# Sparse attention in front of a bilinear feed-forward: probabilities as the stationary operand, and x brought back transposed through DRAM

## Chip, cores and metric

One core of a Trainium2 chip. The metric is the device time of one execution, in microseconds (us). Several executions are timed for each kernel, in the same rounds as the kernel before. "Before" and "after" are the two kernels of the change.

## The reference

```python
# q, k, v: 8 batches x 8 heads x 576 positions x 64, float32
scores = q @ k^T / 8
mask   = local (0 <= i - j < 32) for heads 0-3, strided (j <= i and i % 32 == j % 32) for heads 4-7
attn   = softmax(where(mask, scores, -1e9)) @ v
x      = attn.transpose(0, 2, 1, 3).reshape(4608, 512)
out    = ((x @ w_a) * (x @ w_b)) @ w_out          # 512 -> 1536 -> 512, float32 out
```

The feed-forward contracts over the 512 features. TensorE contracts over partitions, so x has to lie in SBUF transposed, features on partitions (`xT`), before its first matmul.

## The kernel before

Keys and queries are transposed on TensorE, then for each of eight units (a pair of heads, half of the positions) come the scores (S), the masked exponentials `p`, and the values (V). Scores come out keys on partitions, so `p` can be the moving operand and V the stationary one; the result then has features on partitions already and goes straight into `xT`. The price is that the sums over keys have to be made by a matmul with ones, so that they are there for all 64 rows of a head.

```python
def step_S(b, u):                      # scores of one unit, two heads at a time in row halves
    ...
    for i, (k0, q0, g) in enumerate(segs):
        for hh in range(2):
            d0 = 64 * hh
            nc.tensor.matmul(st[:M, hh, i * n:(i + 1) * n],
                             lhsT=kT[d0:d0 + 64, c, k0:k0 + M],
                             rhs=qT[d0:d0 + 64, c, q0:q0 + n], start=True, stop=True)
    ...                                # exp on ScalarE, mask by a bitwise AND on VectorE

def step_V(b, u):                      # sums and values, two heads at a time in column halves
    dn = psm.tile(...)
    for hh in range(2):
        nc.tensor.matmul(dn[64 * hh:64 * hh + 64, :W], lhsT=ones[:M], rhs=p[:M, hh], ...)
    o = psm.tile(...)
    for i, (k0, q0, g) in enumerate(segs):
        for hh in range(2):
            nc.tensor.matmul(o[64 * hh:64 * hh + 64, i * n:(i + 1) * n], lhsT=vt,
                             rhs=p[:M, hh, i * n:(i + 1) * n], ...)
    nc.scalar.activation(ln, dn[:, :W], ACT.Ln)
    nc.scalar.activation(rc, ln, ACT.Exp, scale=-1.0)          # 1 / sum
    nc.vector.tensor_mul(xT[...], o[:, :W], rc)

SEQ = (("T0",), ("S0",), ("S1", "T1"), ("V0", "S2"), ...)       # 13 slots
# the feed-forward of tile t (512 tokens: 12 groups of gate matmuls ffn_ab, 4 of output
# matmuls ffn_y), with one slot of the attention of batch t+1 behind each group
```

Batch 0's attention runs ahead of everything, batch b's is woven into tile b-1, and the last two tiles have none. TensorE, SyncE and GpSimd keep the order in which they are written.

The softmax here doesn't subtract the row's maximum and nothing guards it: scores larger than these inputs give would overflow.

## Time and profile before

| | before |
|---|---|
| median of the runs | 375.85 us |
| first gate matmul of tile 0 (start of the feed-forward) | 25.21 us |
| tile 0, tile 1 | 42.56, 40.89 us |
| tiles 2 to 6, each | 39.95 us |
| tiles 7 and 8, without attention | 31.08 us |

A "tile time" here is the distance from one tile's first gate matmul to the next one's, read from the trace's records. The next fence is from the page of the kernel before: busy tenths of TensorE in 40 slices of the span, and the software DMA queue, which carries the loads (packets, MB, share of the 16 engines' time).

```profile
PE   2789999999999999999999999999999999999995
...
q0 software_dynamic: 46512, 19.67, 43.2%
```

There is no hole in TensorE's row after the first 30 us. To save time, TensorE must be given less to do and must not be made to wait.

### The profile page before, as it was taken

How to read it: one execution, taken by the hardware profiler on the slowest of the kernel's cores; microseconds unless marked ns; L12 is line 12 of the kernel's file. 1: busy time of each engine (PE TensorE's matmuls, PEld its weight loads, DVE VectorE, ACT ScalarE, POOL GpSimd, SP SyncE). 2: the span in 40 equal slices, each digit the busy share in tenths (PEclk: the TensorE clock that was granted, in tenths of full speed). 3: DMA queues.
4: the chain of work that ended last, by engine and by line, in shares of the span. 5: the costliest groups of instructions: out<-in, count | busy, mean ns of one | idle time of the engine just before them, and what ended most of it. 6: DMA issues, size and time to landing. Idle time of an engine off the chain costs nothing.

```text
span 374.7 us, 7708 instructions
## 1 busy us (share of the span) xinstructions
PE 358.7 (96%) x3217; PEld 173.8 (46%) x3217; DVE 169.7 (45%) x299; ACT 178.6 (48%) x347; POOL 52.3 (14%) x72
## 2 busy tenths in 40 slices
PE   2789999999999999999999999999999999999995
PEld 2544454455444544444444544554445444444442
DVE  2653652465426652556245643655255513312421
ACT  1563764466526652666246643766166623312320
POOL 7833540013001110103000300000000000000000
PEclk9999999999999999999999999999999999999999
DMA  7999999845644194229414843000200020011002
GB/s 114 155 194 197 205 191 191 177 66 37 98 117 65 8 100 117 53 40 103 93 56 66 72 81 99 2 2 19 94 2 3 1 86 28 0 58 56 0 30 84
DMA packets 51730, 29.59 MB, mean 79 GB/s; under 512 B 28400, under 2 KB 47088, under 8 KB 51696
## 3 DMA queue, kind: packets, MB, share of 16 engines
q0 software_dynamic: 46512, 19.67, 43.2%
q1 hardware_dynamic: 5184, 9.44, 6.9%
q8 instruction: 25, 0.41, 0.4%
q14 instruction: 9, 0.07, 0.1%
HBM read 39.31 MB, written 9.44 MB: 130 GB/s over the span
## 4 chain that ended last, share of the span: by engine, by line
PE 93%; DMA 2%; POOL 1%; ACT 1%; DVE 1%; issue 1%; DVEq 0%; POOLq 0%
PE mm L254 52%; PE mm L265 25%; PE sm L166 5%; PE st L194 4%; PE sm L213 4%; PE sm L220 2%; DMA vl<-in_v_dram 2%; POOL k L116 0%; DVE y_sb L271 0%; POOL msl L73 0%; ACT rc L226 0%; DVE xT L232 0%; ACT ln L224 0%; POOL q L116 0%; PE mm L166 0%
## 5 line engine op out<-in xcount | busy, mean ns | idle before, releaser
L259 DVE TENSOR_TENSOR pf<-a_sb,mm 128x512 bf16<-128x512 f32 x108 | 74.3, 688 | 89.9 <-PE mm L254 89.9
L254 PE MATMUL mm<-xT,wa_sb 128*128 128x512 bf16 x432 | 113.6, 386 | 0.8 <-DVE xT L232 0.8
L254 PE MATMUL mm<-xT,wb_sb 128*128 128x512 bf16 x432 | 111.9, 382 | 0.0
L258 ACT COPY a_sb<-mm 128x512 f32<-128x512 f32 x108 | 63.2, 585 | 70.2 <-PE mm L254 70.2
L265 PE MATMUL mm<-wo_sb,pf 128*128 128x512 bf16 x432 | 96.3, 379 | 0.0
L254 PEld LDWEIGHTS <-wb_sb 128*128 128x128 bf16 x432 | 42.6, 99 | 52.9 <-issue 2.9
L265 PEld LDWEIGHTS <-pf 128*128 128x128 bf16 x432 | 40.9, 98 | 47.9
L254 PEld LDWEIGHTS <-wa_sb 128*128 128x128 bf16 x432 | 36.4, 98 | 38.4 <-issue 1.7
L199 ACT ACTIVATE p<-st 128x576 bf16<-128x576 f32 (+1 forms) x64 | 40.7, 635 | 17.5 <-PE st L194 17.4
L224 ACT ACTIVATE ln<-sm 128x288 f32<-128x288 f32 x64 | 26.3, 410 | 29.5 <-PE sm L213 29.5
L269 ACT COPY y_sb<-mm 128x512 f32<-128x512 f32 x18 | 10.5, 585 | 56.3 <-PE mm L265 56.3
L271 DVE COPY y_sb<-mm 128x512 f32<-128x512 f32 x18 | 12.5, 692 | 52.9 <-PE mm L265 52.9
L232 DVE TENSOR_TENSOR xT<-sm,rc 128x288 bf16<-128x288 f32 x32 | 20.4, 639 | 28.4 <-ACT rc L226 27.8
L226 ACT ACTIVATE rc<-ln 128x288 f32<-128x288 f32 x64 | 28.3, 443 | 2.0
L172 ACT COPY qT<-sm 128x576 bf16<-128x576 bf16 x28 | 17.8, 637 | 13.9 <-PE sm L166 13.9
L194 PE MATMUL st<-qT,kT 64*72 64x72 bf16 (+1 forms) x448 | 21.1, 212 | 0.6 <-ACT p L199 0.5
L213 PE MATMUL sm<-p,ones 72*64 72x288 bf16 (+1 forms) x128 | 21.1, 327 | 0.3 <-DVE p L205 0.3
L229 DVE TENSOR_TENSOR xT<-sm,rc 128x288 bf16<-128x288 f32 x32 | 14.6, 458 | 14.2 <-ACT rc L226 12.5
L116 POOL DMA_DIRECT2D q<-in_q_dram x16 | 11.7, 730 | 58.4 <-PE sm L166 53.7
L213 PEld LDWEIGHTS <-ones 72*64 72x64 bf16 (+1 forms) x128 | 7.3, 110 | 24.6 <-issue 21.2
L166 PEld LDWEIGHTS <-q 72*64 72x64 bf16 (+1 forms) x448 | 11.2, 117 | 15.9 <-issue 8.9
L129 POOL DMA_DIRECT2D vl<-in_v_dram x8 | 11.6, 1454 | 45.9 <-PE st L194 45.4
(41 smaller groups left out, 177.8 us busy)
## 6 DMA issues: line engine op xcount, KB each, us to landing
out_dram<-y_sb SPq DMA_DIRECT2D x36, 256.0 KB, 2.0
q<-in_q_dram POOLq DMA_DIRECT2D x16, 288.0 KB, 6.8
k<-in_k_dram POOLq DMA_DIRECT2D x16, 288.0 KB, 7.9
vl<-in_v_dram POOLq DMA_DIRECT2D x7, 384.0 KB, 6.8
vs<-in_v_dram POOLq DMA_DIRECT2D x8, 288.0 KB, 5.8
wa_sb<-in_moe_w_a_dram POOLq DMA_DIRECT2D x4, 384.0 KB, 11.6
wb_sb<-in_moe_w_b_dram POOLq DMA_DIRECT2D x4, 384.0 KB, 11.7
wo_sb<-in_moe_w_out_dram POOLq DMA_DIRECT2D x4, 384.0 KB, 13.5
```

The costliest lines, as they stand in the source:

```text
L166: nc.tensor.transpose(tp[64 * hh:64 * hh + 64, r, :], src[:, 2 * cc + hh, r, :], ident[:n, :n])
L172: nc.scalar.copy(o, i_)
L194: nc.tensor.matmul(st[:M, hh, i * n:(i + 1) * n], lhsT=kT[d0:d0 + 64, c, k0:k0 + M], rhs=qT[d0:d0 + 64, c, q0:q0 + n], start=True, stop=True)
L199: nc.scalar.activation(p[:M], st[:M, :, :W], ACT.Exp, scale=scale)
L213: nc.tensor.matmul(dn[64 * hh:64 * hh + 64, :W], lhsT=ones[:M], rhs=p[:M, hh], start=True, stop=True)
L224: nc.scalar.activation(ln, dn[:, :W], ACT.Ln)
L226: nc.scalar.activation(rc, ln, ACT.Exp, scale=-1.0)
L232: nc.vector.tensor_mul(dst, o[:, :W].rearrange("d (r p) -> d p r", r=4), rc.rearrange("d (r p) -> d p r", r=4))
L254: nc.tensor.matmul(ps_, lhsT=w[:, f // FC, kk, 128 * (f % FC):128 * (f % FC + 1)], rhs=xT[:, kk, TTOK * t:TTOK * (t + 1)], start=(kk == 0) ...
L258: nc.scalar.copy(a_sb, ab[0])
L259: nc.vector.tensor_mul(pf[:, f, :], a_sb, ab[1])
L265: nc.tensor.matmul(y, lhsT=pf[:, f, 128 * j:128 * (j + 1)], rhs=wo_sb[:, f, :], start=(f == 0), stop=(f == FD - 1))
```

## The change

The intent is to take work off TensorE. The probabilities become the *stationary* operand and V the moving one. V gets a 65th column of ones, so the sums come out as one more column of the result and the matmuls with ones go away. Scores use whole-array matmuls, with queries padded by zeros, in place of row halves; this avoids changes of tiling. (The tiling is how a matmul divides the array: the views print 128\*128 for the whole array, 64\*128 for a row half, 96\*64 for a column half.) Now the result has positions on partitions, so x must be transposed: for batch 0 on TensorE (X), and from batch 1, the second batch, on by writing the normalized rows to DRAM and reading them back through the DMA crossbar, which transposes on the way (W); this gives TensorE no instruction. Batch 1's attention is pressed into tile 0 by running two slots behind some of the groups.

```diff
-    pmm = ... bufs=4 ...   psm = ... bufs=2 ...
+    pmm = ... bufs=3 ...   po = ... bufs=1 ...   ptp = ... bufs=1 ...   # accumulators
+    dram = ctx.enter_context(tc.tile_pool(name="dram", bufs=2, space=bass.MemoryType.DRAM))
 ...
     def load_vs(b):
-        nc.gpsimd.dma_start(out=t, in_=v[b, HL:].rearrange("h (p r) d -> p h r d", r=RS))
+        for h in range(HL):
+            nc.gpsimd.dma_start(out=vs_buf[b % 2][:, h, :, 0:D], in_=v[b, HL + h]...)
 ...
     def step_S(b, u):
-                nc.tensor.matmul(st[...], lhsT=kT[d0:d0 + 64, c, k0:k0 + M], rhs=qT[d0:d0 + 64, c, q0:q0 + n], ...)
+                nc.tensor.matmul(st[...], lhsT=kT[:, c, k0:k0 + M], rhs=qz[j][:, c, q0:q0 + n], ...)
 ...
     def step_V(b, u):
-            nc.tensor.matmul(dn[...], lhsT=ones[:M], rhs=p[:M, hh], ...)
-                nc.tensor.matmul(o[...], lhsT=vt, rhs=p[:M, hh, i * n:(i + 1) * n], ...)
-        nc.scalar.activation(ln, dn[:, :W], ACT.Ln)
-        nc.scalar.activation(rc, ln, ACT.Exp, scale=-1.0)
+                nc.tensor.matmul(ov[:, j, i, :], lhsT=p[:M, j, i * n:(i + 1) * n], rhs=vt, ...)
+        nc.vector.reciprocal(rc[:n, :, :G], ov[:, :, :, D])
+        nc.vector.tensor_mul(dst, ov[:, :, :, 0:D], rc[...].to_broadcast([n, 2, G, D]))
+
+    def step_X(b, c):                  # batch 0: transpose x on TensorE
+        for g in range(S // n):
+            nc.tensor.transpose(tv[:, g, :], x[:, g].rearrange("p j d -> p (j d)"), ident[:n, :n])
+        nc.scalar.copy(dst, tv)
+
+    def step_W(b, z):                  # other batches: write, then transposing read
+        nc.sync.dma_start(out=xd..., in_=x)
+        nc.sync.dma_start_transpose(out=xT[:, 2 * z:2 * z + 2, S * b:S * (b + 1)], in_=xd)
 ...
+            g0 = 2 if b == 1 else 16 * (b - 1) - 2
+            for b, g0, seq in todo:
+                if seq and i >= g0:
+                    run(b, seq.pop(0))
+                    if b == 1 and i in (3, 4, 12):       # doubled slots
+                        run(b, seq.pop(0))
```

The cuts leave out the layout of the buffers and the new slot order (14 slots, with W0 after the first four units and W1 at the end of each batch).

More of the change, by code (lines that the diff above doesn't have):

```diff
@@ L20 @@
 PAD = 32
+VW = 80
 FC = 3
@@ L52 @@
     nat = ctx.enter_context(tc.tile_pool(name="nat", bufs=2))
-    kvp = ctx.enter_context(tc.tile_pool(name="kv", bufs=2))
     sb = ctx.enter_context(tc.tile_pool(name="sb", bufs=3))
     fsb = ctx.enter_context(tc.tile_pool(name="ffn", bufs=3))
-    pmm = ctx.enter_context(tc.tile_pool(name="pmm", bufs=4, space=bass.MemoryType.PSUM))
+    pmm = ctx.enter_context(tc.tile_pool(name="pmm", bufs=3, space=bass.MemoryType.PSUM))
     pst = ctx.enter_context(tc.tile_pool(name="pst", bufs=1, space=bass.MemoryType.PSUM))
-    psm = ctx.enter_context(tc.tile_pool(name="psm", bufs=2, space=bass.MemoryType.PSUM))
+    po = ctx.enter_context(tc.tile_pool(name="po", bufs=1, space=bass.MemoryType.PSUM))
+    dram = ctx.enter_context(tc.tile_pool(name="dram", bufs=2, space=bass.MemoryType.DRAM))
+    ptp = ctx.enter_context(tc.tile_pool(name="ptp", bufs=1, space=bass.MemoryType.PSUM))
     nc.scalar.preload_act_table_set("natural_log_exp_and_others")
     ident = const.tile([128, 128], BF16)
-    ones = const.tile([128, 64], BF16)
+    qz_buf = [[const.tile([128, KD, S], BF16, name=f"qz{i}{j}") for j in range(2)] for i in range(2)]
+    vl_buf = [const.tile([128, HL * 6, VW], BF16, name=f"vl{i}") for i in range(2)]
+    vs_buf = [const.tile([NP, HL, RS, VW], BF16, name=f"vs{i}") for i in range(2)]
     mask_l = const.tile([128, 4, LW], I16)
@@ L74, in select, with consts @@
                                 channel_multiplier=cm)
-    def consts():
-        nc.vector.memset(ones, 1.0)
-        nc.vector.memset(msl, -1.0)
-        for kT in kT_buf:
-            nc.vector.memset(kT[:, 0:2, 0:PAD], 0.0)
+    def consts(i):
+        if i == 0:
+            nc.vector.memset(msl, -1.0)
+        nc.vector.memset(kT_buf[i][:, 0:2, 0:PAD], 0.0)
+        for j in range(2):
+            nc.vector.memset(qz_buf[i][j][64 * (1 - j):64 * (2 - j)], 0.0)
+        nc.vector.memset(vl_buf[i][:, :, D:D + 1], 1.0)
+        nc.vector.memset(vs_buf[i][:, :, :, D:D + 1], 1.0)
+        if i == 0:
+            nc.vector.memset(vl_buf[0][:PAD, 0, 0:D], 0.0)
     def mask_local():
@@ L119, in load_vl @@
     def load_vl(b):
-        t = nat.tile([128, HL * 6, D], BF16, tag="vl", name="vl")
+        t = vl_buf[b % 2]
         f = 0
@@ L124, in load_vl @@
             f = 1
-            nc.vector.memset(t[:PAD, 0, :], 0.0)
-            nc.gpsimd.dma_start(out=t[PAD:, 0, :], in_=v[0, 0, 0:LW, :])
+            nc.gpsimd.dma_start(out=t[PAD:, 0, 0:D], in_=v[0, 0, 0:LW, :])
         src = bass.AP(tensor=v.tensor, offset=(b * H * S + LW * f - PAD) * D,
                       ap=[[D, 128], [LW * D, HL * 6 - f], [1, D]])
-        nc.gpsimd.dma_start(out=t[:, f:, :], in_=src)
-        nats[b, "vl"] = t.rearrange("p (h w) d -> p h w d", h=HL)
+        nc.gpsimd.dma_start(out=t[:, f:, 0:D], in_=src)
     def load_vs(b):
-        t = nat.tile([NP, HL, RS, D], BF16, tag="vs", name="vs")
-        nc.gpsimd.dma_start(out=t, in_=v[b, HL:].rearrange("h (p r) d -> p h r d", r=RS))
-        nats[b, "vs"] = t
+        for h in range(HL):
+            nc.gpsimd.dma_start(out=vs_buf[b % 2][:, h, :, 0:D],
+                                in_=v[b, HL + h].rearrange("(p r) d -> p r d", r=RS))
     def load_w(src, dst, c):
@@ L147, in load_wo, with step_T @@
         )
-    qkT = {}
-    def step_T(b, c):
-        if b not in qkT:
-            qkT[b] = (kvp.tile([128, KD, S], BF16, tag="qT", name="qT"), kT_buf[b % 2])
-        R, n = (RS, NP) if c >= 2 else (RL, 96)
-        cc = c % 2
-        for i, nm in enumerate(("q", "k")):
-            src = nats[b, nm, c >= 2]
-            dst = qkT[b][i][:, c, :] if i == 0 else qkT[b][i][:, c, PAD:]
-            if b == 0:
-                tp = pmm.tile([128, R, n], BF16, tag="mm", name="mm")
-            else:
-                tp = psm.tile([128, R, n], BF16, tag="sm", name="sm")
-            for r in range(R):
-                for hh in range(2):
-                    nc.tensor.transpose(tp[64 * hh:64 * hh + 64, r, :], src[:, 2 * cc + hh, r, :], ident[:n, :n])
-            if c < 2:
-                o, i_ = dst.rearrange("d (p r) -> d p r", r=R), tp.rearrange("d r p -> d p r")
-            else:
-                o, i_ = dst, tp.rearrange("d r p -> d (r p)")
-            if i == 0 and b > 0:
-                nc.scalar.copy(o, i_)
-            else:
-                nc.vector.tensor_copy(o, i_)
+    def step_T(b, c, nm):
+        src = nats[b, nm, c >= 2]
+        if b == 0:
+            tp = pmm.tile([128, S], BF16, tag="mm", name="mm")
+        else:
+            tp = ptp.tile([128, S], BF16, tag="tp", name="tp")
+        if c < 2:
+            tv = tp.rearrange("d (r p) -> d r p", r=RL)
+            for r in range(RL):
+                for hh in range(2):
+                    nc.tensor.transpose(tv[64 * hh:64 * hh + 64, r, :], src[:, 2 * c + hh, r, :], ident[:96, :96])
+            perm = lambda t: t.rearrange("d (p r) -> d p r", r=RL)
+            tv = tv.rearrange("d r p -> d p r")
+        else:
+            tv = tp.rearrange("d (g p) -> d g p", p=NP)
+            sv = src.rearrange("p h (q r) d -> p h q (r d)", r=2)
+            for g in range(8):
+                nc.tensor.transpose(tv[:, g, :], sv[:, 2 * (c - 2) + g // 4, g % 4, :], ident[:NP, :NP])
+            perm = lambda t: t
+            tv = tp
+        if nm == "k":
+            nc.vector.tensor_copy(perm(kT_buf[b % 2][:, c, PAD:]), tv)
+        else:
+            for j in range(2):
+                pr = slice(64 * j, 64 * j + 64)
+                nc.scalar.copy(perm(qz_buf[b % 2][j][pr, c, :]), tv[pr])
@@ L176, in unit, with step_Tk, step_Tq @@
+    def step_Tk(b, c):
+        step_T(b, c, "k")
+    def step_Tq(b, c):
+        step_T(b, c, "q")
     def unit(u):
         c, half = u // 2, u % 2
-        if c < 2:
-            ws = range(3 * half, 3 * half + 3)
-            return c, half, 128, LW, [(LW * w, LW * w, w) for w in ws]
-        rs = range(4 * half, 4 * half + 4)
-        return c, half, NP, NP, [(PAD + NP * r, NP * r, r) for r in rs]
+        M, n, G = (128, LW, 3) if c < 2 else (NP, NP, 4)
+        segs = [(G * half + i) * n for i in range(G)]
+        return c, half, M, n, G, segs
@@ L185 @@
     ps = {}
     def step_S(b, u):
-        c, half, M, n, segs = unit(u)
-        qT, kT = qkT[b]
+        c, half, M, n, G, segs = unit(u)
+        kT, qz = kT_buf[b % 2], qz_buf[b % 2]
         st = pst.tile([128, 2, 512], F32, tag="st", name="st")
-        for i, (k0, q0, g) in enumerate(segs):
-            for hh in range(2):
-                d0 = 64 * hh
-                nc.tensor.matmul(st[:M, hh, i * n:(i + 1) * n],
-                                 lhsT=kT[d0:d0 + 64, c, k0:k0 + M],
-                                 rhs=qT[d0:d0 + 64, c, q0:q0 + n],
-                                 start=True, stop=True)
+        for i, q0 in enumerate(segs):
+            k0 = q0 + (0 if c < 2 else PAD)
+            for j in range(2):
+                nc.tensor.matmul(st[:M, j, i * n:(i + 1) * n], lhsT=kT[:, c, k0:k0 + M],
+                                 rhs=qz[j][:, c, q0:q0 + n], start=True, stop=True)
@@ L200, in step_S @@
         if c < 2:
-            mk = mask_l[:, half:half + 3].unsqueeze(1).to_broadcast([128, 2, len(segs), n])
+            mk = mask_l[:, half:half + 3].unsqueeze(1).to_broadcast([128, 2, G, n])
         else:
-            mk = mask_s.unsqueeze(1).unsqueeze(1).to_broadcast([NP, 2, len(segs), n])
+            mk = mask_s.unsqueeze(1).unsqueeze(1).to_broadcast([NP, 2, G, n])
         pi = p[:M].bitcast(I16).rearrange("p t (g n) -> p t g n", n=n)
@@ L206, in step_S @@
         ps[b, u] = p
+    xn = {}
     def step_V(b, u):
-        c, half, M, n, segs = unit(u)
+        c, half, M, n, G, segs = unit(u)
         p = ps.pop((b, u))
-        dn = psm.tile([128, 512], F32, tag="sm", name="sm")
-        for hh in range(2):
-            nc.tensor.matmul(dn[64 * hh:64 * hh + 64, :W], lhsT=ones[:M], rhs=p[:M, hh],
-                             start=True, stop=True)
-        o = psm.tile([128, 512], F32, tag="sm", name="sm")
-        for i, (k0, q0, g) in enumerate(segs):
-            for hh in range(2):
-                h = 2 * (c % 2) + hh
-                vt = nats[b, "vl"][:, h, g, :] if c < 2 else nats[b, "vs"][:, h, g, :]
-                nc.tensor.matmul(o[64 * hh:64 * hh + 64, i * n:(i + 1) * n], lhsT=vt,
-                                 rhs=p[:M, hh, i * n:(i + 1) * n],
-                                 start=True, stop=True)
@@ L223, in step_V @@
-        ln = sb.tile([128, W], F32, tag="ln", name="ln", bufs=2)
-        nc.scalar.activation(ln, dn[:, :W], ACT.Ln)
-        rc = sb.tile([128, W], F32, tag="rc", name="rc", bufs=2)
-        nc.scalar.activation(rc, ln, ACT.Exp, scale=-1.0)
-        x = xT[:, c, S * b:S * (b + 1)]
+        o = po.tile([128, 2, 512], F32, tag="o", name="o")
+        ov = o[:n, :, :G * (D + 1)].rearrange("p j (g e) -> p j g e", e=D + 1)
+        for i in range(G):
+            for j in range(2):
+                if c < 2:
+                    vt = vl_buf[b % 2][:, (2 * c + j) * 6 + 3 * half + i, 0:D + 1]
+                else:
+                    vt = vs_buf[b % 2][:, 2 * (c - 2) + half, 2 * i + j, 0:D + 1]
+                nc.tensor.matmul(ov[:, j, i, :], lhsT=p[:M, j, i * n:(i + 1) * n], rhs=vt,
+                                 start=True, stop=True)
@@ L228, in step_V @@
+        rc = sb.tile([128, 2, 4], F32, tag="rc", name="rc")
+        nc.vector.reciprocal(rc[:n, :, :G], ov[:, :, :, D])
+        if u % 4 == 0:
+            xn[b, c // 2] = sb.tile([n, S // n, 4, D], BF16, tag=f"xn{n}", name=f"xn{n}", bufs=2)
+        x = xn[b, c // 2][:, :, 2 * (c % 2):2 * (c % 2) + 2, :]
         if c < 2:
-            nc.vector.tensor_mul(x[:, W * half:W * (half + 1)], o[:, :W], rc)
+            dst = x[:, 3 * half:3 * half + 3].rearrange("p g j d -> p j g d")
         else:
-            dst = x.rearrange("d (p r) -> d p r", r=RS)[:, :, 4 * half:4 * half + 4]
@@ L232, in step_V @@
-            nc.vector.tensor_mul(dst, o[:, :W].rearrange("d (r p) -> d p r", r=4),
-                                 rc.rearrange("d (r p) -> d p r", r=4))
-    SEQ = (("T0",), ("S0",), ("S1", "T1"), ("V0", "S2"), ("V1", "S3"), ("T2",), ("V2", "S4"),
-           ("V3", "S5"), ("T3",), ("V4", "S6"), ("V5", "S7"), ("V6",), ("V7",))
-    FN = {"T": step_T, "S": step_S, "V": step_V}
+            dst = x[:, :, half, :].rearrange("p (g j) d -> p j g d", j=2)
+        nc.vector.tensor_mul(dst, ov[:, :, :, 0:D], rc[:n, :, :G].unsqueeze(3).to_broadcast([n, 2, G, D]))
@@ new lines, in step_X @@
+    def step_X(b, c):
+        x = xn[b, c // 2][:, :, 2 * (c % 2):2 * (c % 2) + 2, :]
+        n = LW if c < 2 else NP
+        if b == 0:
+            tp = pmm.tile([128, S], BF16, tag="mm", name="mm")
+        else:
+            tp = ptp.tile([128, S], BF16, tag="tp", name="tp")
+        tv = tp.rearrange("d (g p) -> d g p", p=n)
+        for g in range(S // n):
+            nc.tensor.transpose(tv[:, g, :], x[:, g].rearrange("p j d -> p (j d)"), ident[:n, :n])
+        dst = xT[:, c, S * b:S * (b + 1)]
+        if c >= 2:
+            dst, tv = dst.rearrange("d (p r) -> d p r", r=RS), tv.rearrange("d g p -> d p g")
+        else:
+            tv = tp
+        nc.scalar.copy(dst, tv)
@@ new lines, in step_W @@
+    def step_W(b, z):
+        xd = dram.tile([S, 4 * D], BF16, tag=f"xd{z}", name=f"xd{z}")
+        x = xn[b, z].rearrange("p g h d -> p g (h d)")
+        if z == 0:
+            nc.sync.dma_start(out=xd.rearrange("(g p) e -> p g e", p=LW), in_=x)
+        else:
+            nc.sync.dma_start(out=xd.rearrange("(p g) e -> p g e", g=RS), in_=x)
+        nc.sync.dma_start_transpose(out=xT[:, 2 * z:2 * z + 2, S * b:S * (b + 1)], in_=xd)
+    SEQ = (("Tk0",), ("Tq0",), ("S0", "Tk1"), ("S1", "Tq1"), ("V0", "S2"), ("V1", "S3", "Tk2"), ("V2", "Tq2"),
+           ("V3", "S4", "W0"), ("S5", "Tk3"), ("V4", "Tq3"), ("V5", "S6"), ("S7",), ("V6",), ("V7", "W1"))
@@ L239, in run @@
+    FN = {"Tk": step_Tk, "Tq": step_Tq, "S": step_S, "V": step_V, "X": step_X, "W": step_W}
     def run(b, slot):
         for s in slot:
-            FN[s[0]](b, int(s[1]))
+            FN[s[:-1]](b, int(s[-1]))
     pfs = {}
@@ L247, in ffn_ab @@
         if f == 0:
-            pfs[t] = fsb.tile([128, FD, TTOK], BF16, tag="pf", name="pf", bufs=2)
+            pfs[t] = fsb.tile([128, FD, TTOK], BF16, tag="pf", name="pf", bufs=1)
         pf = pfs[t]
@@ L277 @@
         load_qk(0, False)
-        consts()
+        consts(0)
         make_identity(nc, ident)
@@ L283 @@
         load_vl(0)
-        for slot in (("T0",), ("T1",), ("S0",)):
+        for slot in (("Tk0",), ("Tq0",), ("Tk1",), ("S0",), ("Tq1",), ("S1",)):
             run(0, slot)
@@ L291 @@
         load_qk(1, False)
+        consts(1)
         load_vl(1)
@@ L300 @@
             load_wo(c)
-        for slot in (("S1",), ("T2",), ("V0",), ("S2",), ("V1",), ("S3",), ("T3",), ("V2",),
-                     ("S4",), ("V3",), ("S5",), ("V4",), ("S6",), ("V5",), ("S7",), ("V6",), ("V7",)):
+        for slot in (("Tk2",), ("V0",), ("S2",), ("Tq2",), ("V1",), ("S3",), ("Tk3",), ("V2",), ("X0",), ("S4",),
+                     ("Tq3",), ("V3",), ("S5",), ("V4",), ("X1",), ("S6",), ("V5",), ("S7",), ("V6",), ("X2",),
+                     ("V7",), ("X3",)):
             run(0, slot)
+        slots = []
         for t in range(NT):
-            steps = list(SEQ) if t + 1 < B else []
-            slots = [lambda f=f: ffn_ab(t, f) for f in range(FD)] + [lambda j=j: ffn_y(t, j) for j in range(4)]
-            first = 3 if t == 0 else 0
-            for i, grp in enumerate(slots):
-                grp()
-                if t + 2 < B:
-                    if i == 2:
-                        load_qk(t + 2, False)
-                    elif i == 5:
-                        load_vl(t + 2)
-                    elif i == 8:
-                        load_qk(t + 2, True)
-                    elif i == 11:
-                        load_vs(t + 2)
-                if steps and i >= first:
-                    run(t + 1, steps.pop(0))
+            slots += [(ffn_ab, t, f) for f in range(FD)] + [(ffn_y, t, j) for j in range(4)]
+        todo = []
+        for b in range(1, B):
+            g0 = 2 if b == 1 else 16 * (b - 1) - 2
+            todo.append((b, g0, list(SEQ)))
+        loads = {}
+        for b in range(2, B):
+            g0 = 16 * (b - 2)
+            loads[g0 + 1] = lambda b=b: load_qk(b, False)
+            loads[g0 + 5] = lambda b=b: load_vl(b)
+            loads[g0 + 8] = lambda b=b: load_qk(b, True)
+            loads[g0 + 11] = lambda b=b: load_vs(b)
+        for i, (fn, t, j) in enumerate(slots):
+            fn(t, j)
+            if i in loads:
+                loads[i]()
+            for b, g0, seq in todo:
[3 more added lines that the diff above has]
+                        run(b, seq.pop(0))
 _INS = ['q', 'k', 'v', 'moe_w_a', 'moe_w_b', 'moe_w_out']
```

## The prediction

> **What bounds the kernel now.** I read the page first (engine shares, the slices, the chain of waits), then the chain in order of time, then the timeline of TensorE for one tile in the middle and for the first 45 us, then the DMA view of the whole run and of its first 75 us.
>
> ```profile
> PE 358.7 (96%) x3217; PEld 173.8 (46%) x3217; DVE 169.7 (45%) x299; ACT 178.6 (48%) x347; POOL 52.3 (14%) x72
> DMA  7999999845644194229414843000200020011002
> PE 93%; DMA 2%; POOL 1%; ACT 1%; DVE 1%; issue 1%; DVEq 0%; POOLq 0%
> ```
>
> TensorE is busy 96% and carries 93% of the chain; VectorE and ScalarE are under half. What is not issued on TensorE is won, anything else only if TensorE waits for it. The DMA row says that the engines are full in the first 70 us and mostly free later.
>
> ```profile
> 71.23 1.83 PE mm L254 x8
> ...
> 111.18 1.83 PE mm L254 x8
> ...
> 308.58 20.72 PE mm L254 x96
> 329.30 10.36 PE mm L265 x48
> 339.66 20.72 PE mm L254 x96
> ```
>
> In the chain, a tile of 512 tokens with one batch's attention woven in takes 111.18 - 71.23 = 39.95 us; one without (the last two) takes 339.66 - 308.58 = 31.08. So a batch of attention costs TensorE 8.87 us, and only that can shrink. The next fence is the middle of such a tile.
>
> ```profile
> 70.53 0.45 PE L166 MATMUL sm<-ident,q 96*64 96x96 bf16 x12
> 70.81 0.42 PE L166 MATMUL sm<-ident,k 96*64 96x96 bf16 x12
> 71.16 1.04 PE L254 MATMUL mm<-xT,wa_sb 128*128 128x512 bf16 x4
> 72.03 1.03 PE L254 MATMUL mm<-xT,wb_sb 128*128 128x512 bf16 x4
> 72.99 0.30 PE L194 MATMUL st<-qT,kT 64*128 64x96 bf16 x6
> 73.23 1.04 PE L254 MATMUL mm<-xT,wa_sb 128*128 128x512 bf16 x4
> ...
> 80.19 0.31 PE L213 MATMUL sm<-p,ones 128*64 128x288 bf16 x2
> 80.34 0.29 PE L220 MATMUL sm<-p,vl 128*64 128x96 bf16 x6
> 80.56 0.30 PE L194 MATMUL st<-qT,kT 64*128 64x96 bf16 x6
> 80.80 1.04 PE L254 MATMUL mm<-xT,wa_sb 128*128 128x512 bf16 x4
> ```
>
> Single records inside these rows: the half-array matmuls of a pair start 3 ns apart and the next pair 42 ns later (N=96; 32 ns for N=72), so pairs do run side by side. From the last one's start to the next matmul of another tiling are 134 to 138 ns, of which 40 are its streaming: every change of tiling costs about 97 ns. The score group shows it: 72.99 to 73.23 is 0.24 us, three pairs (0.13) and one change; another lies ahead of it (72.03 to 72.99 is 0.96 where four matmuls take 4 x 0.2165 = 0.87).
>
> **What the skill says.** "TensorEngine Tiling (Array Packing)", Key Properties: "Mode switching requires drain". The trace agrees: 97 ns. "TensorE: Matmul & The Clock Gate", Back-to-back issue gap: N/2.4 + 2.5 ns. That gives 216, 42.5 and 32.5 ns for N = 512, 96 and 72, and the trace has 216, 42 and 32. The same page, LDWEIGHTS: P/1.2 ns for P columns, 80 ns for 96. The trace speaks against that as a throughput: 64-column loads, two to a pair, keep up with pairs every 32 ns, so a load runs at 2 columns per ns or better beside a matmul. "DMA: Bandwidth & Descriptors", Latency and other measured facts: 261 GB/s for a crossbar transpose whose middle dimension is not contiguous. No run here shows a transpose yet.
>
> **The change part by part, per batch.** With N=96 in 0.0425 us and N=72 in 0.0325:
>
> Now: transposes of the local heads 24 pairs x 0.0425 = 1.02; of the strided heads 32 x 0.0325 = 1.04; scores 12 x 0.0425 + 16 x 0.0325 = 1.03; sums 8 x 0.143 (80.19 to 80.34) = 1.14; values 1.03. Together 5.26. The 13 slots hold 33 changes of tiling: 33 x 0.097 = 3.2. Sum 8.46, against 8.87 measured, so the model misses some 0.03 us a slot.
>
> After: local transposes 1.02, still in column pairs, in 4 slots with a change before and after each, 8 x 0.097 = 0.78; strided 32 whole transposes of two heads, 1.04; scores 24 x 0.0425 + 32 x 0.0325 = 2.06, doubled because zero-padded queries give up the row pairs; the sums vanish (a column of ones in V); values with P stationary stream 65 columns (29.6 ns), but the load of 96 or 72 columns is longer and I take it as the pitch, 24 x 0.0425 + 32 x 0.0325 = 2.06. The crossbar takes the rest off TensorE. Sum 6.96, with a few small losses 7.15. **Gain about 1.7 us a batch, 7 batches: 12 us.** Utilization of the array halves, yet 25 changes of tiling and the sums go.
>
> Other engines, hidden if the order holds. ScalarE loses Ln and Exp (8 x 0.85) and gains a second query copy (4 x 0.64). VectorE gains reciprocals (estimate 8 x 0.15) and longer multiplies (384 or 512 elements, estimate 0.56 to 0.69 from 0.458 at 288). Of the matmul accumulators there are 3 instead of 4. Walking one tile through the built order with the old durations, I find every accumulator free 0.8 us or more before its next use, and scores, values and query copies ready 0.3 to 0.6 us ahead. So no stall there.
>
> **What it gives back, at the start.**
>
> ```profile
> 14.00 0.45 PE L220 MATMUL sm<-p,vl 128*64 128x96 bf16 x5 [1.81 <-DMA vl<-in_v_dram]
> ...
> 25.21 1.89 PE L254 MATMUL mm<-xT,wa_sb 128*128 128x512 bf16 x4
> ```
> ```profile
> out_dram<-y_sb SPq DMA_DIRECT2D x36, 256.0 KB, 2.0
> ```
> ```profile
> out_dram<-y_sb SPq DMA_DIRECT2D x4, 256.0 KB, 5.8
> ```
>
> Batch 0 runs alone, at half clock (four N=512 matmuls in 1.7 us, not 0.87). Its first values wait until 14.0 for the load of v, and the feed-forward starts at 25.2: eight units of 1.4 us. After, the output accumulator is single, so a unit is: values 0.67 to completion, reciprocal 0.15, multiply 0.6, with masks and key copies between, and four transposes of x on TensorE besides (0.48 each at half clock). Followed instruction by instruction, this starts the feed-forward at about 28.1, **2.9 us later**. Four memsets of 1152 words (about 1 us each, from 0.38 for 384) end before the first keys land at 7.6.
>
> Batch 1 is pressed into tile 0 with doubled slots: scores right behind the query transposes that they need (two copies of 0.6: wait 1.3), the same again for the second pair of heads (1.25), and V7 right behind V6 on one accumulator (0.85). Before has 0.8 of such waits. **Net 2.5 us later.**
>
> Batch 1's second crossbar trip leaves at about 66 and is wanted at about 73. The two last fences are the DMA view over the whole run and over its first 75 us: an output store takes 2.0 us in general and 5.8 while the loads queue. Write plus transpose of 295 KB may take 8 to 12 there: **a stall of 0 to 6 us, I take 1.5**, low, because I suppose that the doubled slots were made to cover it.
>
> From the third batch on the last trip leaves some 10 us ahead of its use: store about 3, transpose 2 us fixed plus 1.1 at 261 GB/s (estimate on the skill's figure), beside the next v load, in all about 7 to 8. Hidden.
>
> Sum: 375.85 - 12 + 2.9 + 2.5 + 1.5 = 370.8. The denser start may lift the clock earlier (the first five microseconds of feed-forward lose 2.5 us to it now); I credit 1.8. **Predicted 369 us.**
>
> **The rivals.** First, weight loads are not hidden behind such short matmuls: values and strided scores then cost load plus stream (40 + 30 and 30 + 32 ns), about +2.5 us a batch, time about 386. Against it: loads hidden behind 32 ns today. For it: today's are half-array loads, and P/1.2 would be slower still. I give it 8%. Second, the crossbar trip is late in every tile: 2 us x 6 more, about 381, showing as TensorE waiting for a transpose into x at each tile's third matmul; for it, the trip was never measured here and 128-byte v packets share the queue; 12%. Third, only batch 1's trip is late, 6 us and a half-clock restart: about 375; for it, the full DMA row; 20%. Fourth, the clock rises in batch 0 and batch 1's trip is just in time: about 365. Weight arrival is no rival: the weights for the last quarter of tile 0 land 5 us ahead of use and the start moves later.
>
> **Range and chances.** The gain of 12 us is nearly arithmetic; the refunds at the start, 2 to 11 us, are not. So 363 to 376 holds it 8 times in 10. Two per cent is 368.3, just inside my centre: faster 0.42, within 0.50, slower 0.08.
>
> **What would show it.** Right: a tile in the middle takes 38.1 to 38.4 us; scores and values groups take 0.25 to 0.27 us with no gap to the matmuls around them; the last two tiles stay at 31.08; the feed-forward starts at 27 to 29; waits of some 1.3 us at batch 1's first scores. Wrong: values groups of 0.4 us or more (loads exposed); a wait for a DMA into x at each tile; waits of the feed-forward for a_sb or pf (three accumulators too few).

## The result, and the profile after

After: 381.23 us (median of 4 runs, 380.5 to 382.05). Before, in the same rounds: 375.57 us (375.12 to 375.96). The ratio is 1.015, 95% interval 1.012 to 1.018. A ratio here is the mean time of one kernel's runs over the mean of the other's of the same rounds, so it is not quite the ratio of the medians quoted. The change makes the kernel 1.5% slower: within 2%, but outside the predicted range of 363 to 376.

First, the page of the kernel after: engine shares, the slices of TensorE, of its granted clock and of the DMA engines, the software queue, and the chain's shares.

```profile
PE 349.0 (92%) x2813; PEld 189.0 (50%) x2861; DVE 181.5 (48%) x366; ACT 158.5 (42%) x259; POOL 72.6 (19%) x96
...
PE   1869798829999999999999999999999999999996
...
PEclk9999999958999999999999999999999999999999
DMA  7999999995596449934983499111501140011002
...
q0 software_dynamic: 68400, 19.69, 56.1%
...
PE 87%; DMA 6%; DVE 2%; issue 1%; POOL 1%; ACT 1%; DVEq 0%; ACTq 0%; POOLq 0%
```

TensorE's busy time did fall, by 9.7 us as printed, and the whole span grew by 5.5 us (374.7 to 380.2). The trace of after lacks 48 matmul records of the feed-forward (2813 matmuls beside 2861 weight loads), and the short gaps that they leave, 2.3 us in all, count as not busy. So the fall is nearer 7.4 us, and some 13 us more than before pass with TensorE not busy. The row of TensorE shows where: an 8 and a 2 in the eighth and ninth slice, 67 to 86 us, with a dip of the clock in the ninth and tenth. DMA, 2% of the chain before, is 6% now. The software queue moves the same bytes in half as many packets again.

The chain of waits, in order of time, names the hole (start, duration, what):

```profile
65.71 0.70 DVE xn L245
...
66.42 6.83 DMA xd<-xn
...
73.27 10.10 DMA xT<-xd
83.42 2.72 PE mm L293 x6
```

The last values of batch 1 are normalized at 66.4 us. Their write to DRAM takes 6.83 us, the transposing read 10.10, and only then does tile 1 go on: 17 us of round trip. The timeline of TensorE (start, length of the group, line, operation, in brackets the idle time ahead and what ended it) shows the same from TensorE's side, with the start of the feed-forward above and a tile in the middle below:

```profile
28.83 1.49 PE L293 MATMUL mm<-xT,wa_sb 128*128 128x512 bf16 x3 [0.22 <-issue]
30.11 1.91 PE L293 MATMUL mm<-xT,wb_sb 128*128 128x512 bf16 x4
...
33.40 1.03 PE L293 MATMUL mm<-xT,wb_sb 128*128 128x512 bf16 x4
...
83.42 1.01 PE L293 MATMUL mm<-xT,wa_sb 128*128 128x512 bf16 x2 [9.03 <-DMA xT<-xd]
84.22 1.91 PE L293 MATMUL mm<-xT,wb_sb 128*128 128x512 bf16 x4
...
88.38 1.03 PE L293 MATMUL mm<-xT,wb_sb 128*128 128x512 bf16 x4
...
123.38 1.04 PE L293 MATMUL mm<-xT,wa_sb 128*128 128x512 bf16 x4
...
130.04 0.42 PE L234 MATMUL o<-vl,p 128*96 128x65 bf16 x6
130.30 0.42 PE L209 MATMUL st<-qz,kT 128*128 128x96 bf16 x6
130.55 1.03 PE L293 MATMUL mm<-xT,wa_sb 128*128 128x512 bf16 x4
...
161.72 1.04 PE L293 MATMUL mm<-xT,wa_sb 128*128 128x512 bf16 x4
```

Tile 1 has room for its first two matmuls only (features 0 to 255, from the first trip), then waits 9.03 us for features 256 to 511. Afterwards four matmuls take 1.91 us in place of 1.03: the clock had dropped during the wait. The trace's clock records, which the views show only as means, have half clock from 77.65 to 87.89 us and full clock on both sides. In the middle, 161.72 - 123.38 = 38.34 us a tile, 1.61 less than before; a values group and a scores group follow each other in 0.26 and 0.25 us without a gap.

Why the trip takes so long is in the DMA engines' row for 66 to 85 us, after and then before. A digit is the busy tenth of one of 40 slices of the window. The second line of the first fence gives the time from issue to landing of the one transpose issued in it.

```profile
DMA  9999999999999999999999999997999999999999
...
xT<-xd SPq DMA_TRANSPOSE x1, 10.1
```
```profile
DMA  9999999998778873000000008599999821000000
```

Before, the queue of loads has run dry at about 74 us, and the later burst is short. After, the engines are full through the whole window. It is no longer the weights, which had landed by 56.3 us, but the last of batch 2's loads (landed by 70.9), then batch 3's (issued from 60.9 on, landed by 87.0), beside batch 1's trip and the output stores. Before, the same loads of batch 3 were issued from 48.7 on and had landed by 74.3. From 250 to 310 us, where nothing is left to load, the same two transfers take this:

```profile
xd<-xn SPq DMA_DIRECT2D x4, 288.0 KB, 2.7
...
xT<-xd SPq DMA_TRANSPOSE x4, 3.5
```

So a trip takes 2.7 + 3.5 = 6.2 us on idle engines, and 17 us at batch 1's end.

Tile by tile, the difference adds up. One correction is in it: the first group of the feed-forward after shows three matmuls of four and 0.22 us of "issue", so one record is missing; in x1 and hold3 below, where it is there, it starts 0.47 us after the transposes ahead, which makes it 27.95 + 0.47 = 28.42 here.

| | before | after | difference |
|---|---|---|---|
| feed-forward starts | 25.21 | 28.42 | +3.21 |
| tile 0 | 42.56 | 45.57 | +3.01 |
| tile 1 | 40.89 | 49.39 | +8.50 |
| tiles 2 to 5, together | 159.81 | 153.36 | -6.45 |
| tile 6 | 39.95 (to 308.42) | 37.39 | -2.56 |
| tiles 7 and 8 | 31.08 each | the same | 0 |
| sum | | | +5.71 |

The spans differ by 5.5. Tile 1 alone turns a gain into a loss. Tile 6 gains more than the others because an attention starts two groups ahead of its tile now; the first two transposes of batch 2 lie in tile 0.

Tile 0 can be taken apart too. It is 45.57 - 38.34 = 7.2 us longer than a tile in the middle. The doubled slots leave three holes in TensorE's timeline: 2.13 us from the first query transposes to the end of the scores behind them, where the same groups take 0.73 elsewhere; 2.19 for 0.89 at the second pair of heads; 1.76 for 0.55 at V6 and V7. That is 3.9 us. The first 12 matmuls at half clock, 28.42 to 33.40, cost 4.98 - 12 x 0.2165 = 2.4. Batch 2's two transposes add about 0.95, what tile 6 is shorter by. The sum is 7.2. In the kernel before, the view of waits lists none in tile 0, and its 16 slow matmuls (25.21 to 31.28) cost 6.07 - 16 x 0.2165 = 2.6, all that sets tile 0 apart from the middle there. Its tile 1 is 0.9 us longer than the middle: after three matmuls it waits 0.77 us, at 69.36, for the last multiply into `xT`.

### The profile page after: what moved, and what is told of

Read it like the earlier page. It is cut to its first block, busy times and chain, and to the rows that moved or that the text cites. A ratio compares the mean times of both kernels' runs of the same rounds, so it can differ in the third digit from the quotient of the medians.

```text
span 380.2 us, 6884 instructions
## 1 busy us (share of the span) xinstructions
PE 349.0 (92%) x2813; PEld 189.0 (50%) x2861; DVE 181.5 (48%) x366; ACT 158.5 (42%) x259; POOL 72.6 (19%) x96
## 3 DMA queue, kind: packets, MB, share of 16 engines
q0 software_dynamic: 68400, 19.69, 56.1%
## 4 chain that ended last, share of the span: by engine, by line
PE 87%; DMA 6%; DVE 2%; issue 1%; POOL 1%; ACT 1%; DVEq 0%; ACTq 0%; POOLq 0%
PE mm L293 50%; PE mm L304 22%; PE o L234 5%; PE st L209 4%; DMA xT<-xd 3%; PE tp L170 3%; PE tp L177 2%; DMA vl<-in_v_dram 2%; DMA xd<-xn 2%; DVE xn L245 1%; ACT p L212 1%; ACT qz L185 1%; POOL k L126 0%; POOL msl L78 0%; DVE rc L237 0%
## 5 line engine op out<-in xcount | busy, mean ns | idle before, releaser
L298 DVE TENSOR_TENSOR pf<-a_sb,mm 128x512 bf16<-128x512 f32 x108 | 74.3, 688 | 101.6 <-PE mm L293 73.5
L293 PE MATMUL mm<-xT,wa_sb 128*128 128x512 bf16 x412 | 109.5, 386 | 10.4 <-DMA xT<-xd 9.0
L293 PEld LDWEIGHTS <-wa_sb 128*128 128x128 bf16 x432 | 37.3, 100 | 43.3 <-issue 11.3
L185 ACT COPY qz<-tp 64x576 bf16<-64x576 bf16 x56 | 35.4, 631 | 29.8 <-PE tp L170 17.9
L245 DVE TENSOR_TENSOR xn<-o,rc 96x384 bf16<-96x384 f32 (+1 forms) x64 | 39.6, 619 | 1.9
L308 ACT COPY y_sb<-mm 128x512 f32<-128x512 f32 x18 | 10.6, 586 | 69.7 <-PE mm L304 69.7
L234 PEld LDWEIGHTS <-p 72*72 72x72 bf16 (+1 forms) x448 | 28.6, 127 | 16.9 <-DVE xn L245 4.8
L209 PE MATMUL st<-qz,kT 128*72 128x72 bf16 (+1 forms) x448 | 30.2, 212 | 3.0 <-ACT qz L185 2.8
L142 POOL DMA_DIRECT2D vs<-in_v_dram x32 | 25.8, 809 | 28.9 <-PE o L234 17.7
L209 PEld LDWEIGHTS <-kT 128*72 128x72 bf16 (+1 forms) x448 | 25.7, 116 | 10.1 <-issue 3.7
L181 DVE COPY kT<-tp 128x576 bf16<-128x576 bf16 x28 | 16.9, 603 | 15.8 <-PE tp L170 15.8
L138 POOL DMA_DIRECT2D vl<-in_v_dram x8 | 11.6, 1456 | 33.5 <-PE st L209 31.1
L234 PE MATMUL o<-vs,p 72*72 72x65 bf16 x256 | 15.1, 205 | 3.0 <-DVE xn L245 3.0
L218 DVE TENSOR_TENSOR p<-p,mask_s 72x576 int16<-72x576 int16 x32 | 14.3, 447 | 3.4 <-ACT p L212 3.4
## 6 DMA issues: line engine op xcount, KB each, us to landing
vs<-in_v_dram POOLq DMA_DIRECT2D x32, 72.0 KB, 10.1
```

The lines of the kernel that those rows point to most:

```text
L142: nc.gpsimd.dma_start(out=vs_buf[b % 2][:, h, :, 0:D], in_=v[b, HL + h].rearrange("(p r) d -> p r d", r=RS))
L181: nc.vector.tensor_copy(perm(kT_buf[b % 2][:, c, PAD:]), tv)
L185: nc.scalar.copy(perm(qz_buf[b % 2][j][pr, c, :]), tv[pr])
L209: nc.tensor.matmul(st[:M, j, i * n:(i + 1) * n], lhsT=kT[:, c, k0:k0 + M], rhs=qz[j][:, c, q0:q0 + n], start=True, stop=True)
L218: nc.vector.tensor_tensor(pi, pi, mk, op=ALU.bitwise_and)
L234: nc.tensor.matmul(ov[:, j, i, :], lhsT=p[:M, j, i * n:(i + 1) * n], rhs=vt, start=True, stop=True)
```

## The experiments

Two theories of the loss stood against each other. **A**: it is batch 1's late trip, made long by the loads in the same DMA engines, with what follows (the clock). **B**: it is the compression of batch 1 into tile 0, and the new operations themselves. Further runs test parts of the accounting: the size of the crossbar's gain, the cost of a change of tiling, and the start. They ran in three sessions: x1, hold3, x1_pairs and x1_single against before at 375.58 us, x1_whole3, x_all, x1_two and best at 375.93, best_warm at 375.86 (medians of 7 runs each). Between sessions, compare the ratios or the tile times rather than the medians.

**x1: batch 1's x on TensorE.** No trip through DRAM for batch 1; four groups of transposes on TensorE take its place in tile 0.

```diff
+    SEQ1 = (... ("V3", "S4", "X0"), ("S5", "Tk3"), ("V4", "Tq3"), ("V5", "S6", "X1"), ("S7",), ("V6",), ("V7", "X2"), ("X3",))
-            todo.append((b, g0, list(SEQ)))
+            todo.append((b, g0, list(SEQ1 if b == 1 else SEQ)))
```

> Batch 1 brings its normalized rows back with TensorE transposes in the same slots, no crossbar trip for it. Theory A (the whole slip beyond the forecast is batch 1's second trip, which meets full DMA engines): TensorE's 9.0 us wait for a DMA into x at tile 1 goes, and the 1.9 us that it loses afterwards at half clock; four transposes add 1.0: 371.3 us, 370 to 373. Rival B (the DMA engines are so late by then that the next thing that needs them waits instead: batch 2's queries, or the output stores): the wait moves, 376 us or more. Tiles in the middle stay at 38.34 us in both.

Measured: 372.10 us (371.13 to 372.85), ratio 0.990 [0.987, 0.993]. Tile 0 grew by 1.2 us (46.75), tile 1 fell to 38.34. Theory A stands: without the trip tile 1's loss is gone.

**hold3: the trip kept, the loads beside it held back.** GpSimd, which issues the loads, first reads one column of x that the trip brings. Nothing else is moved.

```diff
+        def hold(b):
+            if b == 3:
+                nc.gpsimd.tensor_copy(gate, xT[:, 3, 2 * S - 1:2 * S])
-            loads[g0 + 1] = lambda b=b: load_qk(b, False)
+            loads[g0 + 1] = lambda b=b: (hold(b), load_qk(b, False))
```

> Crossbar trips all kept; the loads of batch 3 are held back (GpSimd reads an element of x that batch 1's second trip writes) so that no load runs beside the transpose of that trip. Theory A1 (the trip is slow because loads share the DMA engines): that transpose falls from 10.1 us to 3.5 to 5, as in the last two batches where nothing is loading, the wait of tile 1 from 9.0 to 0 to 2, time 370 to 373 us. Rival A2 (a crossbar transpose of this size takes some 10 us by itself, and 3.4 is special to the last batches): transpose stays at 9 us or more, wait 6 us or more, time 378 us or more.

Measured: 370.61 us (369.82 to 371.01), ratio 0.986 [0.984, 0.988]. That is 10.6 us faster than after, by one instruction. The DMA row for 66 to 76 us and the landing time of the transpose:

```profile
DMA  9999999997742110000000699999999970039948
...
xT<-xd SPq DMA_TRANSPOSE x1, 3.3
```

The engines run empty in the middle of the window, and the transpose of the same 288 KB now takes 3.3 us in place of 10.1. It could be issued 4.2 us after the write ahead of it (66.0 to 70.2), in place of 6.85; the loads issued before the hold had landed by 68.6. Tile 1 has no wait left (38.33 us). This settles the cause: the trip was long because of the loads queued beside it. What it costs is the wait of 9.0 us plus the half clock after it, about 2.0 us.

**x1_single: no doubled slots.** x1 with batch 1 starting one group earlier and one slot behind each group, so that compression is gone.

```diff
-            g0 = 2 if b == 1 else 16 * (b - 1) - 2
+            g0 = 1 if b == 1 else 16 * (b - 1) - 2
-                    if b == 1 and i in (3, 4, 12):
-                        run(b, seq.pop(0))
-        if b == 0:
+        if b == 0 or c >= 2:              # in step_X: x's last transposes use another accumulator
```

> As x1, but batch 1's attention begins one slot earlier and takes one slot a step, without the doubled slots; its last two transposes use the feed-forward's accumulators. Theory: the waits for query copies (0.72 + 0.46 + 0.49 + 0.46 us) and of V7 behind V6 (1.02) in tile 0 go: 3 us under x1, 368 us. Rival (they only move to other places of tile 0, or the loads of batch 1 aren't in yet): under 1 us.

Measured: 367.12 us (366.78 to 367.67), ratio 0.978 [0.975, 0.980], 5.0 us below x1. Tile 0 takes 41.60. More than expected: the view of waits lists none in tile 0 now, for holes of 3.9 us as worked out above, and the clock also came up at about 31.1 us in place of 34.0 in x1, which is worth 1.2 (8 slow matmuls that lose 1.26 us in place of 12 that lose 2.5). Together 5.1, and tile 0 shrank by 46.75 - 41.60 = 5.15. (The part of the clock may be chance: see x1_two.) So theory B was true in part: it is the smaller part of the loss beside the trip's 11, and the doubled slots lose time whatever happens to x.

**x_all: x on TensorE for every batch.** x1_single with the order that has X for all batches; no crossbar at all.

```diff
-            todo.append((b, g0, list(SEQ1 if b == 1 else SEQ)))
+            todo.append((b, g0, list(SEQ1)))
```

> As x1_single, but no crossbar trip at all: every batch turns its rows with TensorE transposes. Theory (from batch 2 on the trips lie beside other work and save TensorE 1.04 us a batch): tile 39.4 us, six batches, 6.2 us over x1_single: 373.3 us. Rival (the trips cost elsewhere, in DMA contention or waits for output tiles, as much as they save): 367 to 369 us.

Measured: 374.44 us (373.70 to 375.19), ratio 0.996 [0.993, 0.998]; a middle tile takes 39.38. Against 38.34, the crossbar is worth 1.04 us a batch, 6.2 us over the six batches. The medians lie 7.3 us apart, but across two sessions, and in the profiled execution x_all also started its feed-forward 0.7 us later and got its full clock at 34.25 us for 30.65. Of the 1.61 us that a middle tile gains in the change, 39.95 - 39.38 = 0.57 is P stationary with all that belongs to it, and 1.04 is the crossbar.

**x1_pairs: scores back to row halves.** x1 with 64-row scores: the number of scores' matmul passes halves, and the changes of tiling come back.

```diff
+                pr = slice(64 * j, 64 * j + 64)
-                nc.tensor.matmul(st[...], lhsT=kT[:, c, k0:k0 + M], rhs=qz[j][:, c, q0:q0 + n], ...)
+                nc.tensor.matmul(st[...], lhsT=kT[pr, c, k0:k0 + M], rhs=qz[j][pr, c, q0:q0 + n], ...)
```

> As x1, but the scores go back to two half-array matmuls side by side (row pairs) in all batches. Theory (a change of tiling costs 97 ns): scores save 1.03 us a batch, 14 more changes of tiling cost 1.36: 0.33 us a batch slower, tile 38.7 us, 2 to 3 us over x1. Rival (the array's halved use is what counts): 1.03 us a batch faster, tile 37.3 us, 7 us under x1.

Measured: 374.35 us (374.25 to 374.41), ratio 0.996 [0.995, 0.998], 2.25 us above x1; a middle tile takes 38.80, not 38.34. TensorE's timeline of the place that answers to 130.04 above:

```profile
119.83 0.42 PE L235 MATMUL o<-vl,p 128*96 128x65 bf16 x6
120.19 0.30 PE L210 MATMUL st<-qz,kT 64*128 64x96 bf16 x6
```

Values to scores is 0.36 us in place of 0.26, the 0.1 us of one change of tiling. Half as many array passes lose to the changes around them, so the padded scores are right here.

**x1_whole3: whole-array transposes of the local heads.** x1_single with two heads side by side in a row of the loaded q and k, from batch 3 on, so that a transpose takes 128 columns whole. The loads were laid anew, six per tensor.

```diff
+                for r in range(R):
+                    nc.gpsimd.dma_start(out=t[:, r], in_=src[b, h0:h0 + HL].rearrange("h (p r) d -> r p h d", r=R)[r])
 ...
+                if b >= 3:
+                    nc.tensor.transpose(tv[:, r, :], src[:, r, 2 * c:2 * c + 2, :].rearrange("p h d -> p (h d)"), ident[:96, :96])
+                    continue
```

> As x1_single, but from batch 3 on the local q and k are loaded with the heads of a pair beside each other, so that their transposes too use the whole array: no change of tiling is left in those batches. Theory (97 ns a change, 8 changes a batch): 0.78 us a batch off, tile 37.56 us in place of 38.34, five batches, 3.9 us under x1_single: 363.2 us. Rival (the loads in 256-byte runs arrive late, or the drain is paid elsewhere): 366 us or more.

Measured: 363.51 us (363.08 to 364.35), ratio 0.967 [0.965, 0.969]. A tile with such a batch takes 37.45 us, 0.89 less, for eight changes of tiling removed: 0.11 us each. TensorE has no other kind of tiling left there.

**x1_two: batch 0 without its single accumulator.** x1_single, in batch 0 with every second unit's values in two accumulators of the feed-forward.

```diff
+        if b == 0 and u % 2:
+            os_ = [pmm.tile([128, 512], F32, tag="mm", name="mm") for j in range(2)]
+            parts = ...                   # one head of the pair each; reciprocal and multiply twice
```

> As x1_single, but in batch 0 every second unit of values writes to two spare accumulators, so that it need not wait for the multiply of the unit before. Theory (the start is late because values, reciprocal and multiply of one unit chain to the next through one accumulator): the feed-forward starts at 26.6 us in place of 28.1, 1.5 us under x1_single: 365.6 us. Rival (TensorE at half clock or scores to exp to mask bind the start): under 0.5 us.

Measured: 367.46 us (367.18 to 367.82), ratio 0.977 [0.975, 0.979]: no gain over 367.12, a miss. The feed-forward did start earlier, 27.29 for 28.09, but the clock came up at about 33 us for 31.1, and tile 0 took 43.16 for 41.60. In the profiled execution, what was won ahead of the clock's rise was lost behind it. Why it rises at one moment and not another was not tested, but the clock records of the traces narrow it down. In all eleven traces every record but the last lasts a whole multiple of 3.413 us (101 of these in before; 13, 3 and 86 in after; 2, 5 and 96 in best_warm), so the clock changed only at the ends of such periods. Its first rise without warm-up lies anywhere from 30.53 us (before) to 34.25 (x_all): at 30.65 in x1_single, 32.36 in hold3, 33.03 in x1_two and 34.01 in x1, and batch 0 is the same work in x1_single, hold3 and x1. Where the periods fall in the one execution profiled may thus decide the clock's part of x1_single's gain and of x1_two's miss; no run here separates that.

**best: x1_whole3 and x1_two together.**

> x1_whole3 and x1_two together. If their gains add: 361.7 us, some 3.7% under the kernel before.

Measured: 362.71 us (362.25 to 363.44), ratio 0.965 [0.962, 0.967]. The edit is the sum of the two above. It is 3.5% faster than before; its lead of 0.8 us over x1_whole3 is small beside their ranges (363.08 to 364.35).

**best_warm: a warm clock for batch 0.** best with 16 matmuls on a filled tile at the very start.

```diff
+        warm = const.tile([128, TTOK], BF16, name="warm")
+        nc.vector.memset(warm, 0.5)
+        wt = pst.tile([128, 2, 512], F32, tag="st", name="st")
+        for i in range(16):
+            nc.tensor.matmul(wt[:, 0, :], lhsT=warm[:, 0:128], rhs=warm, start=True, stop=True)
```

> As the combined kernel, with 16 useless 128x512 matmuls while TensorE waits for the first loads. Theory (the slow start of TensorE is a clock that rises only after some microseconds of steady matmuls, and batch 0's own work, with its waits, is not steady enough to raise it): the matmuls before 7 us end with starts 216 ns apart; if batch 0 then holds the clock, the feed-forward starts at full rate at 25 to 26 us and the time is 358 to 360; if it falls again in batch 0's waits, the time stays within 0.7 us of the combined kernel's 362.7. The first says what the forecast's credit for an earlier clock would have needed.

Measured: 362.39 us (362.14 to 363.68), ratio 0.965 [0.963, 0.968]: the same as best. The view by windows shows why (window, length, busy time of PE, PEld, DVE, ACT and POOL, then granted clock, DMA and GB/s):

```profile
8.00:14.00 6.00, 3.13 (x75) 2.54 (x74) 3.37 (x10) 3.72 (x6) 2.62 (x4) 1.00 1.42 125
14.00:20.00 6.00, 5.65 (x81) 5.30 (x79) 4.00 (x14) 4.34 (x8) 6.00 (x10) 0.51 1.35 107
```

The clock was up from 7.34 us and fell to half at 14.17: TensorE was busy for only half of 8 to 14 us, with a wait of 1.26 us for v among it. Batch 0's chain of small steps did not hold the clock; it came back at 31.24 us.

## Why the prediction was wrong, step by step

**What held.** The gain of a middle tile was to be 1.7 us, at 38.1 to 38.4; it is 1.61, at 38.34. Values and scores groups take 0.25 to 0.27 us, so the first rival, exposed weight loads, is refuted. The middle tiles' last trips are hidden, as predicted, and the second rival is refuted: batch 3's is issued at 151.94 and by the trace's packet records its transpose ends at 159.8, 7.8 us for 7 to 8 predicted, and it is wanted at about 162.2, so it left 10 us ahead, as predicted too. (Each batch's first trip has more room: its transpose takes 9 to 11 us beside the loads, and batch 3's had landed at 153.0.) The last two tiles stay at 31.08. The start of the feed-forward moved by 3.2 us for 2.9 predicted.

**The step that failed** is the term "a stall of 0 to 6 us, I take 1.5" for batch 1's second trip. Write and transpose were estimated at 8 to 12 us from the store that took 5.8 among the loads; they took 6.83 + 10.10 = 17 us. Tile 1 is 49.39 - 38.34 = 11.05 us longer than a tile in the middle: the wait of 9.0, and about 2.0 at half clock after it, which the term did not hold at all. "Low, because I suppose that the doubled slots were made to cover it" put a guess in the place of an estimate. The trip leaves at 66.4 as predicted and is wanted at 74.4, so the order covers 8 us and no more. The third rival had the mechanism, late trip and half-clock restart, but only 6 us for it and a chance of 20%.

**Two smaller terms failed in tile 0.** The waits of the compressed batch 1 were put at 2.5 us net: 1.3, 1.25 and 0.85, less 0.8 that before had. The listed waits came close (1.18, 0.95 and 1.02), but the holes around them are longer, 3.9 in all; less the 0.9 that before lost at the head of its tile 1, that is 3.0 net. And the credit of 1.8 us for an earlier rise of the clock brought 0.2 (2.4 us lost in place of 2.6). best_warm shows batch 0 losing a clock that it had been given.

Put right, with what the terms measured: 369.0, + 9.5 for the trip (11.05 for 1.5), + 0.5 for the waits (3.0 for 2.5), + 1.6 for the clock, + 0.3 for the start, + 0.7 for seven gains of 1.61 in place of 12 us. That is 381.6, counted from before at 375.85; from 375.57, its median in the rounds of the result, it is 381.3, and 381.23 was measured.

**What stays open**: why the loads keep the engines full to 85 us after, when before they had run dry at about 74. hold3 shows that the loads make the trip long, not which property of them. The amount is the same (19.69 and 19.67 MB on the load queue), and it is not the trip itself: x1 has none for batch 1 and x_all none at all, and their engines stay full to about 80 and 82 us. In x_all the packets of the load queue, 68400 in place of 46512, take 51.5% of 373.4 = 192 us of the engines' time for 43.2% of 374.7 = 162 before. That speaks for the shorter v packets; but v also comes by four issues a batch in place of one, and no run separates the two.

## What to carry to other kernels

A transfer's latency was not a property of the transfer here: the same 288 KB took 3.3 to 11.1 us to transpose, by what was queued with it in the shared engines. Where a result goes out to memory and back, find the one trip with the least slack and the fullest queue, and time it there; the others being hidden says nothing of it, and holding back a load that nobody needs yet was worth about as much as all the work saved (10.6 us by one instruction; seven batches of 1.61 are 11.3). And count changes of tiling before counting array passes: 0.1 us each decided both scores and transposes here.

## What the Trainium skill lacked or had wrong

- "DMA: Bandwidth & Descriptors", Latency and other measured facts, gives a rate for a crossbar transpose but nothing for one that shares the engines with a full load queue: the same 288 KB took 3.3 to 3.5 us alone and 10.1 us beside the loads, and the write ahead of it 2.7 and 6.8 us.
- "Advanced Engine Details and Errata", X-Bar Transpose (TRN2), says "TRN2 transpose DMAs are as fast as regular DMAs". On idle engines the transpose took 3.5 us and the write of the same bytes 2.7; over the landings that the trace gives (8 of the 14 transposes, most of them beside loads, and 7 of the 14 writes) the medians are 9.4 and 4.4.
- "TensorE: Matmul & The Clock Gate", LDWEIGHTS, gives P/1.2 ns, 80 ns for 96 columns. Whole-array values with a new 96-column stationary operand for each matmul ran at 42 to 43 ns each on average (six in 0.255 us), so loads keep up at twice that rate. The record of one such load lasts 124 ns on average in tile 2, so loads overlap each other, and neither figure is the pace.
- "TensorE: Matmul & The Clock Gate", Part 1: The HAM clock gate, puts the slow clock "after ≥1 idle window (~3.4µs)"; it also names micro-idle times between groups of matmuls as a cause, but no number for either says how idle is idle. In best_warm the clock fell at the end of 3.41 us (10.76 to 14.17) in which TensorE was busy for 1.47 us and no wait was longer than 1.26 us. No page says that the profile's granted-clock row reads full where the trace has no clock record yet: in before the records begin at 30.53 us, and the slices ahead of it read 9 while four N=512 matmuls take 1.9 us.
- "TensorEngine Tiling (Array Packing)", Key Properties, has no figure for the drain at a change of mode: 97 ns from before's records, and 0.11 us each from the eight changes that x1_whole3 removed.
